# Transposing the layers' operands by DMA, token by token, instead of on TensorE

## The chip, the cores and the metric

The kernel runs on one core of a Trainium2 chip. The metric is device time in microseconds (us); lower is better. Three executions of the kernel before took 1181.19, 1182.12 and 1182.57 us, median 1182.12 us.

## The reference

Top-32 attention over 4 batches, 8 heads, 576 positions and 64 dimensions; its output, 2304 tokens by 512, passes through two layers with 2048 hidden columns each.

```python
scores = scale * np.matmul(q, k.transpose(0, 1, 3, 2))
kth = np.partition(scores, -top_k, axis=-1)[..., -top_k:-top_k + 1]
scores = np.where(scores >= kth, scores, -1000000000.0)
...
x = attention.transpose(0, 2, 1, 3).reshape(B * S, H * D)      # 2304 x 512
h = np.maximum(x @ moe_w_in, 0.0);  x = (h * h) @ moe_w_out    # first layer
h = x @ moe2_w_in                                             # second layer
out = (h * np.clip(h + 3.0, 0.0, 6.0) / 6.0) @ moe2_w_out
```

q, k and v are float32; the four weight matrices arrive as float64.

## The kernel before, in words

Every product keeps more than half precision: an operand is scaled by a power of two and split into two float16 parts, high and low, and a product is high*high + high*low + low*high, three matmuls for one (`PRODS`).

The 2304 tokens are cut into 20 blocks (four of 128 tokens and one tail of 64 in each batch), and these into 18 units of 128 tokens; two units consist of two tails each. Attention goes by tiles: 144 of them, eight for a block (one head each) or four for a tail (two heads each). A tile (`attend`) is scores on TensorE (line 769), their copy on ScalarE (775), seven VectorE passes for the 32 largest (783, 788, 791), a mask on GpSimd (808), the exponential on ScalarE (813), its two parts (819, 823, 824), a transposing DMA into wT (828), and 14 small matmuls with v (842).

When the tiles of a block are done, `x_operand` makes the first layer's input: ScalarE copies the block out of PSUM (912), four float32 transposes on TensorE turn it (921), ScalarE squares it (927), four matmuls with ones16 add the squares over the 512 columns, token by token (932), VectorE takes the largest (936) and a power of two from it (263 to 265), ScalarE scales (965) and rounds (968), GpSimd subtracts (971). That fills the tile hl of the unit: columns on partitions, tokens along the free axis.

A layer (`group`, m is 0 or 1) runs in four groups of four slices f of 128 hidden columns. For a slice, `up` makes 12 matmuls of 128x128 (1091): the hidden columns of 128 tokens. After the four slices follow the activation on ScalarE (and VectorE in the second layer), rounding (1113) and subtraction (1116) into ghl. Then `acc` multiplies by the second matrix, again slice by slice. In the second layer ghl is stationary and 512 columns of the weight move, three matmuls a slice (1134). In the first layer the weight is stationary, block by block, and the 128 tokens of ghl move: 12 matmuls a slice (1126), so that its result stands with columns on partitions, as the second layer's input must stand. `x2_operand` then squares it (1010), adds up (1016), scales (1028, 1029) and splits it (275, 279) straight from PSUM into hl, over the first input.

The order of the work is not that of the source. Every step is a task with an engine, an assumed cost, the tasks it needs, and the buffers that it takes and frees. `Plan.run` goes through them as through events in time; when an engine is free it takes, of the tasks that are ready and whose buffers are free, the one with the smallest key, `offset + slope * position` from the table `PRIO`. The engines run what comes out, each strictly in that order, and so does the queue of SyncE (SP), which issues all DMAs. A task of SP has latency 2.0 in the plan, the transposes into wT have `WLAT = 4.5`.

Of the kernel before, what the change touches and what calls it, by code (L numbers as in the profile page):

```python
# [134 lines left out]
def tile_topk_attention_moe_moe2(  # L135
# [36 lines left out]
    ones16 = const.tile([P, P], BF16, name="ones16")  # L172
    nc.gpsimd.memset(ones16, 1.0)
# [57 lines left out]
    pool("ghl", GBUFS, [P, 2, 512], F16)  # L231
    pool("m", 4, [P, TOPK], F32, st)
# [3 lines left out]
    for name, n in (("nb", NBUFS), ("kb", 2), ("ss", 6), ("sck", 1), ("scv", 1), ("scq", 2), ("qinv", 2), ("xy", 2), ("scx", 6),  # L236
                    ("px", 6), ("sc2", 4), ("p2", 2), ("r", 6), ("pm", 2), ("sm", 2), ("ca", 2), ("oc", 2)):
        scalar(name, n)
# [645 lines left out]
    def x_operand(i):  # L884
# [21 lines left out]
        def copy():  # L906
            box["x"] = x = take("x")
            a_ = T["av", i]
            for t in range(ntl):
                for hh in range(2 if tail else 1):  # L910
                    rows = slice(hh * TAIL, hh * TAIL + TAIL) if tail else slice(0, P)
                    nc.scalar.activation(x[0:n, 2 * t + hh if tail else t, :], a_[rows, t * D:(t + 1) * D], AF.Copy,  # L912
                                         scale=box["rv"][rows, t:t + 1])

        def flip():
            if o == 0:
                T["hl", u] = take("hl")
            box["pt"] = take("misc", "pt").rearrange("p (c n) -> p c n", c=KD)[:, :, 0:n]
            x = box["x"].rearrange("p h d -> p (h d)")
            for c in range(KD):  # L920
                nc.tensor.transpose(box["pt"][:, c, :], x[0:n, c * P:(c + 1) * P], ident[0:n, 0:n])

        def part(a):
            return T["hl", u][:, a, :, o:o + n]

        def square():
            nc.scalar.activation(part(1).bitcast(BF16), box["pt"], AF.Square)

        def total():
            box["pn"] = take("h", "pnx")[:, 0:n]  # L930
# [3 lines left out]
        def scale():  # L934
            y = take("xy")
            nc.vector.tensor_reduce(y, box["pn"], axis=AX.X, op=ALU.max)
            T["sx", i], T["px", i] = take("scx"), take("px")
            scale_pair(y, T["px", i], EXP_P, T["sx", i])
# [6 lines left out]
        t3 = task("ACT", 1.6, ("xcopy", first[i]), copy, deps=[t2, *avs], alloc=["x"])  # L945
        free("rv", t1, t3)
        free("av", avs[0], t3)
        t4 = task("PE", 0.44 if not tail else 0.3, ("xflip", first[i]), flip, deps=[t3, hl_task.get(u)],
                  alloc=["misc"] + (["hl"] if o == 0 else []))
        hl_task.setdefault(u, t4)  # L950
        free("x", t3, t4)
        t5 = task("ACT", act(4 * n), ("xsquare", first[i]), square, deps=[t4])
        t6 = task("PE", mm(KD, n), ("xtotal", first[i]), total, deps=[t5], alloc=["h"])
        t7 = task("DVE", 0.65, ("xscale", first[i]), scale, deps=[t6], alloc=["xy", "scx", "px"])
        free("h", t6, t7)
        free("xy", t7, t7)
        scale_task[i] = t7
        if (SX if i else SX0) == "d":
            l_, = split(4 * n, lambda: box["pt"], [lambda: part(0)], [lambda: part(1)], lambda: T["sx", i], "d",
                        (("xhigh", first[i]), ("xlow", first[i])), [t7])  # L960
            free("misc", t4, l_)
        else:
            def evac():
                box["y"] = take("f", "y").rearrange("p (c n) -> p c n", c=KD)[:, :, 0:n]
                nc.scalar.activation(box["y"], box["pt"], AF.Copy, scale=T["sx", i])

            def high():
                nc.scalar.activation(part(0), box["y"], AF.Copy)

            def low():  # L970
                nc.gpsimd.tensor_tensor(part(1), box["y"], part(0), op=ALU.subtract)

            t8 = task("ACT", act(4 * n) + 0.09, ("xevac", first[i]), evac, deps=[t7], alloc=["f"])
            free("misc", t4, t8)
            t9 = task("ACT", act(4 * n), ("xhigh", first[i]), high, deps=[t8])
            l_ = task("POOL", gps(4 * n), ("xlow", first[i]), low, deps=[t9])
            free("f", t8, l_)
        opd_task.setdefault((0, u), []).append(l_)

    def x2_operand(u):  # L980
# [19 lines left out]
        def bank(i):  # L1000
            w_ = P if n == P else 2 * P
            return acc_t.rearrange("p b n -> p (b n)")[:, 0:KD * w_].rearrange("p (c n) -> p c n", c=KD)[
                :, :, off[i]:off[i] + nof[i]]

        def part(i, a):
            return T["hl", u][:, a, :, off[i]:off[i] + nof[i]]

        def square(i):
            box["ss", i] = take("ss")
            nc.scalar.activation(part(i, 1).bitcast(BF16), bank(i), AF.Square, accum_out=box["ss", i],  # L1010
                                 **({"scale": T["px", i]} if several else {}))

        def total():
            box["pn"] = take("h", "pnx")[:, 0:1]
            for i in us:
                nc.tensor.matmul(box["pn"], ones32, box["ss", i], start=i == us[0], stop=i == us[-1])
# [15 lines left out]
        if several:  # L1032
# [3 lines left out]
            for i in us:  # L1036
                free("scx", scale_task[i], t1, *opd_task[0, u])
        sq = [task("ACT", act(4 * nof[i]), ("ysquare", pos[1, u, 0]), lambda i=i: square(i), deps=[t1, acc_task[0, u]], alloc=["ss"])
              for i in us]
        t3 = task("PE", 0.25, ("ytotal", pos[1, u, 0]), total, deps=sq, alloc=["h"])  # L1040
        for t_ in sq:
            free("ss", t_, t3)
# [3 lines left out]
        for i in us:  # L1046
            lows += split(4 * nof[i], lambda i=i: bank(i), [lambda i=i: part(i, 0)], [lambda i=i: part(i, 1)],
                          lambda i=i: T["px", i] if several else box["s"], "d", (("yhigh", pos[1, u, 0]), ("ylow", pos[1, u, 0])), [t4])
        opd_task[1, u] = lows
# [10 lines left out]
        for b_ in range(1 if n == P else 2):  # L1060
            free(f"acc{b_}", acc_task["first", 0, u], *lows)
# [10 lines left out]
    def group(m, u, g):  # L1072
# [45 lines left out]
        def acc(fi, chunks):  # L1118
            f = g * GF + fi
            gl = [box["g"][:, d, fi * n:(fi + 1) * n] for d in range(2)]  # L1120
            if m == 0:
                w_ = P if n == P else 2 * P
                flat_ = acc_t.rearrange("p b n -> p (b n)")
                for c in range(KD):
                    for a, d in PRODS:
                        nc.tensor.matmul(flat_[:, c * w_:c * w_ + n], wt[1][:, f, a, c * P:(c + 1) * P], gl[d],  # L1126
                                         start=(f, a, d) == (0, 0, 0) and c * w_ % 512 == 0,
                                         stop=f == KF - 1 and (a, d) == PRODS[-1], skip_group_check=True)
            else:
                for ch in chunks:  # L1130
                    rows = min(P, n - ch * P)
                    o_ = acc_t[0:rows, 1 if n == P else ch, :]
                    for a, d in PRODS:
                        nc.tensor.matmul(o_, gl[d][:, ch * P:ch * P + rows], wt[3][:, f, a, :],  # L1134
# [300 lines left out]
```

## Time and profile before

| | |
|---|---|
| median of three executions | 1182.12 us |
| the profiled execution | 1180.5 us, span 1178.7 us |
| PE (matmuls) | 1051.4 us busy, 89% |
| DVE | 988.8 us, 84% |
| ACT | 925.6 us, 79% |
| POOL | 835.3 us, 71% |
| mean granted TensorE clock | 0.979 |

The span runs from the first to the last instruction; the execution lasts 1.8 us longer. An engine's busy time is the time in which at least one of its instructions is shown; a matmul's length contains the way through the array, so the distance from one start to the next tells what it costs when they follow closely. The first 200 us, in which the weights are converted, and the last 80 us differ from what lies between.

### The profile page before, as it was taken

Reading aid. Unit: us, or ns where it says so; the run is one execution under the profiler, and the core shown is the slowest. Engines: PE = TensorE matmul, PEld = TensorE weight load, DVE = VectorE, ACT = ScalarE, POOL = GpSimd, SP = SyncE. Lnnn points to the kernel's source line nnn. Section 1 sums busy time; section 2 is a strip of 40 time slices with the busy share of each in tenths; the row PEclk is TensorE's granted clock in tenths of the full one; section 3 lists DMA queues with packets and bytes.
Section 4 is the critical chain, followed back from the end, with each engine's and each line's share of the span. In section 5 each row is a group of like instructions: output and inputs, shape, how many; then the busy total and the mean of one; then the engine's idle time right before and its main releaser. Section 6 shows DMA issues by size and latency. Waiting matters only on the chain.

```text
span 1178.7 us, 36919 instructions
## 1 busy us (share of the span) xinstructions
PE 1051.4 (89%) x14792; PEld 862.5 (73%) x14792; DVE 988.8 (84%) x2319; ACT 925.6 (79%) x1868; POOL 835.3 (71%) x1113
## 2 busy tenths in 40 slices
PE   2375688878999999999999999999989999999998
PEld 1232336776788788889787978888777978888885
DVE  4989899998995999999989999999978999998101
ACT  6589599899798878788888878888887787877432
POOL 5858868699775677777867787786766778777321
PEclk9997699988999999999999999999999999999999
DMA  9888754423554343445464443445463334333100
GB/s 235 234 249 244 225 156 119 104 48 65 90 97 102 79 75 55 75 74 98 78 118 84 71 74 56 72 62 92 86 110 55 66 65 80 62 60 61 12 11 19
DMA packets 276764, 112.50 MB, mean 95 GB/s; under 512 B 257520, under 2 KB 265712, under 8 KB 276592
## 3 DMA queue, kind: packets, MB, share of 16 engines
q1 hardware_dynamic: 276592, 110.14, 45.2%
q8 instruction: 116, 1.90, 0.7%
q14 instruction: 56, 0.46, 0.1%
HBM read 48.23 MB, written 4.72 MB: 45 GB/s over the span
## 4 chain that ended last, share of the span: by engine, by line
PE 53%; ACT 18%; DVE 9%; POOL 8%; issue 6%; DMA 5%; SPq 1%; ACTq 0%; DVEq 0%; POOLq 0%
PE hb L1091 21%; PE acc L1134 12%; PE acc L1126 11%; PE sp L769 4%; PE av L842 3%; POOL E L808 2%; ACT E L813 2%; DVE W L788 2%; ACT x L912 2%; POOL wc L823 2%; ACT S L775 2%; DVE m L791 1%; DVE cv L364 1%; DMA kT<-kn 1%; ACT w L541 1%
## 5 line engine op out<-in xcount | busy, mean ns | idle before, releaser
L1091 PE MATMUL hb<-hl,w 128*128 128x128 f16 x6912 | 456.2, 219 | 4.8 <-ACT stg L410 1.4
L1091 PEld LDWEIGHTS <-w 128*128 128x128 f16 x6912 | 411.4, 98 | 50.7 <-issue 6.4
L791 DVE MAX8 m<-W 128x8 f32<-128x576 f32 x432 | 326.0, 755 | 8.3
L1126 PE MATMUL acc<-ghl,w 128*128 128x128 f16 x3456 | 243.5, 221 | 5.3 <-ACT ghl L1113 2.6
L1134 PE MATMUL acc<-w,ghl 128*128 128x512 f16 x864 | 231.5, 379 | 11.7 <-DVE hl L279 7.5
L808 POOL TENSOR_TENSOR E<-S,E 128x576 f32<-128x576 f32 x144 | 204.3, 1419 | 48.5 <-ACT E L805 42.1
L1116 POOL TENSOR_TENSOR ghl<-r,ghl 128x512 f16<-128x512 f32 x144 | 169.4, 1177 | 93.5 <-ACT ghl L1113 85.3
L1126 PEld LDWEIGHTS <-w 128*128 128x128 f16 x3456 | 209.7, 99 | 17.6 <-issue 7.0
L788 DVE MATCH_REPLACE8 W<-m,W 128x576 f32<-128x576 f32 x288 | 213.8, 742 | 0.0
L823 POOL TENSOR_TENSOR wc<-E,wc 128x512 f16<-128x512 f32 x144 | 168.0, 1166 | 39.6 <-ACT wc L819 39.0
L775 ACT ACTIVATE S<-sp 128x576 f32<-128x576 f32 x144 | 93.5, 649 | 48.1 <-POOL E L808 40.0
L813 ACT ACTIVATE E<-E,scalars,scl 128x576 f32<-128x576 f32 x144 | 125.1, 869 | 4.4 <-POOL E L808 4.3
L805 ACT ACTIVATE E<-S,scalars 128x576 f32<-128x576 f32 x144 | 111.8, 776 | 19.0 <-DVE scalars L800 14.9
L783 DVE MAX8 m<-S 128x8 f32<-128x576 f32 x144 | 107.9, 750 | 18.9 <-ACT S L775 18.3
L769 PE MATMUL sp<-kT,qT 128*128 128x288 f16 (+1 forms) x640 | 100.1, 298 | 24.8 <-ACT S L775 20.0
L1134 PEld LDWEIGHTS <-ghl 128*128 128x128 f16 x864 | 74.9, 99 | 56.0 <-issue 16.0
L788 DVE MATCH_REPLACE8 W<-m,S 128x576 f32<-128x576 f32 x144 | 107.0, 743 | 0.0
L1106 DVE SCALAR_TENSOR_TENSOR r<-r,hb 128x512 f32<-128x512 f32 x72 | 49.0, 680 | 67.6 <-ACT r L1100 66.7
L1113 ACT ACTIVATE ghl<-r 128x512 f16<-128x512 f32 x144 | 90.5, 629 | 17.4 <-DVE r L1106 12.6
L819 ACT ACTIVATE wc<-E 128x576 f16<-128x576 f32 x144 | 98.5, 684 | 1.3
L795 POOL TENSOR_SCALAR scalars<-m,scl 128x1 f32<-128x1 f32 x144 | 38.5, 269 | 81.5 <-ACT E L813 32.2
L769 PEld LDWEIGHTS <-qT 128*128 128x128 f16 (+1 forms) x640 | 54.9, 103 | 51.8 <-issue 34.4
(130 smaller groups left out, 1493.5 us busy)
## 6 DMA issues: line engine op xcount, KB each, us to landing
w<-in_moe_w_in_dram SPq DMA_DIRECT2D x32, 512.0 KB, 4.9
w<-in_moe_w_out_dram SPq DMA_DIRECT2D x29, 512.0 KB, 4.4
out_dram<-o SPq DMA_DIRECT2D x16, 256.0 KB, 2.1
qf<-in_q_dram SPq DMA_DIRECT2D x31, 128.0 KB, 2.7
stg<-in_k_dram SPq DMA_DIRECT2D x12, 256.0 KB, 2.9
stg<-in_v_dram SPq DMA_DIRECT2D x12, 256.0 KB, 3.2
wT<-wc SPq DMA_TRANSPOSE x144, 3.2
stg<-in_moe_w_out_dram SPq DMA_DIRECT2D x6, 256.0 KB, 3.3
```

Source lines behind the costliest of these rows:

```text
L769: nc.tensor.matmul(dst, qT[:, 2 * ((2 * hp + hh) % 4) + a, 0:M], kflat[:, hh * SPAD + c * HALF:hh * SPAD + (c + 1) * HALF], start=a == 0, ...
L775: nc.scalar.activation(T["S", s].rearrange("p (c n) -> p c n", c=2), T["sp", s][:, :, 0:HALF], AF.Copy)
L788: nc.vector.match_replace(out=T["W", s], in_to_replace=m[:, 8 * c - 8:8 * c], in_values=T["S", s] if c == 1 else T["W", s], imm_value=-3.0e38)
L791: nc.vector.max(m[:, 4 * r:4 * r + 8], T["W", s])
L805: nc.scalar.activation(T["E", s], T["S", s], AF.Relu, bias=T["kb", s], scale=-FAR)
L808: nc.gpsimd.tensor_tensor(T["E", s], T["S", s], T["E", s], op=ALU.subtract)
L813: nc.scalar.activation(T["E", s], T["E", s], AF.Exp, bias=T["nb", s], scale=T["scl", ("q", i, half)][:, hp % 2:hp % 2 + 1], accum_out=T["s ...
L823: nc.gpsimd.tensor_tensor(wc[:, S + TAIL:], e[:, 0:S - TAIL], wc[:, 0:S - TAIL], op=ALU.subtract)
L1091: nc.tensor.matmul(box["h"][:, fi * n:(fi + 1) * n], wt[2 * m][:, kk * 4 + f // 4, a, f % 4 * P:(f % 4 + 1) * P], hl[:, c, kk, 0:n], start ...
L1116: nc.gpsimd.tensor_tensor(flat(box["g"][:, 1]), flat(box["r"]), flat(box["g"][:, 0]), op=ALU.subtract)
L1126: nc.tensor.matmul(flat_[:, c * w_:c * w_ + n], wt[1][:, f, a, c * P:(c + 1) * P], gl[d], start=(f, a, d) == (0, 0, 0) and c * w_ % 512 == ...
L1134: nc.tensor.matmul(o_, gl[d][:, ch * P:ch * P + rows], wt[3][:, f, a, :], start=f == 0 and (a, d) == (0, 0), stop=f == KF - 1 and (a, d) = ...
```

## The change

Both operands are now split while tokens lie on partitions, and turned afterwards by one transposing DMA for each (128 tokens x 2 parts x 512 columns, float16).

In `x_operand` the four TensorE transposes go. ScalarE squares the copied block in SBUF with a sum along each row (a reading of the accumulator more), one small float32 matmul with ones32 adds over the tokens (the sum of all squares takes the place of the largest), the VectorE reduction goes, the block is scaled in place, rounded, subtracted into the new buffer xh, and SP issues the transpose from xh into hl. In `acc` the first layer now does as the second: ghl stationary, 512 weight columns moving, three matmuls a slice. In `x2_operand` the split writes xh too, and a second transposing DMA fills hl. There is one buffer xh; of wT there are two instead of three. hl is taken at the copy and no longer at the transpose. The table PRIO has other numbers in every row, and so the order of all engines is another one; two of its rows are shown.

```diff
-    ones16 = const.tile([P, P], BF16, name="ones16")
-    nc.gpsimd.memset(ones16, 1.0)
...
+    pool("xh", XHBUFS, [P, 2, 512], F16)
...
+        def square():
+            box["xh"] = take("xh")
+            box["ss"] = take("ss")
+            nc.scalar.activation(box["xh"][0:n, 0].bitcast(BF16), rows(), AF.Square, accum_out=box["ss"][0:n])
+
+        def total():
+            box["pn"] = take("misc", "pnx")[:, 0:1]
+            nc.tensor.matmul(box["pn"], ones32[0:n, :], box["ss"][0:n], start=True, stop=True)
...
+        def scaled():
+            nc.scalar.activation(rows(), rows(), AF.Copy, scale=T["sx", i][0:n])
+
+        def high():
+            nc.scalar.activation(box["xh"][0:n, 0], rows(), AF.Copy)
+
+        def low():
+            nc.gpsimd.tensor_tensor(box["xh"][0:n, 1], rows(), box["xh"][0:n, 0], op=ALU.subtract)
+
         def flip():
-            if o == 0:
-                T["hl", u] = take("hl")
-            box["pt"] = take("misc", "pt").rearrange("p (c n) -> p c n", c=KD)[:, :, 0:n]
-            x = box["x"].rearrange("p h d -> p (h d)")
-            for c in range(KD):
-                nc.tensor.transpose(box["pt"][:, c, :], x[0:n, c * P:(c + 1) * P], ident[0:n, 0:n])
...
-            for c in range(KD):
-                nc.tensor.matmul(box["pn"], ones16, part(1).bitcast(BF16)[:, c, :], start=c == 0, stop=c == KD - 1)
...
+            nc.sync.dma_start_transpose(out=T["hl", u].rearrange("p a c n -> p (a c) n")[:, :, o:o + n],
+                                        in_=box["xh"][0:n].rearrange("p a n -> p (a n)"))
...
+        l_ = task("SP", 1.25, ("xflip", first[i]), flip, deps=[t10], lat=WLAT)
+        free("xh", t5, l_)
...
+        def flip():
+            nc.sync.dma_start_transpose(out=T["hl", u].rearrange("p a c n -> p (a c) n"),
+                                        in_=box["yh"].rearrange("p a n -> p (a n)"))
...
+            lows += split(DM, lambda r=rows(i): acc_t[r, 0, :], [lambda r=rows(i): box["yh"][r, 0]],
+                          [lambda r=rows(i): box["yh"][r, 1]], lambda i=i: (T["px", i] if several else box["s"])[rows(i)],
+                          "d", (("yhigh", pos[1, u, 0]), ("ylow", pos[1, u, 0])), [t4])
+        t6 = task("SP", 1.25, ("yflip", pos[1, u, 0]), flip, deps=lows, lat=WLAT)
...
-            if m == 0:
-                w_ = P if n == P else 2 * P
-                flat_ = acc_t.rearrange("p b n -> p (b n)")
-                for c in range(KD):
-                    for a, d in PRODS:
-                        nc.tensor.matmul(flat_[:, c * w_:c * w_ + n], wt[1][:, f, a, c * P:(c + 1) * P], gl[d],
...
+            o_ = acc_t[0:n, m, :]
+            for a, d in PRODS:
+                nc.tensor.matmul(o_, gl[d], wt[2 * m + 1][:, f, a, :], start=f == 0 and (a, d) == (0, 0),
+                                 stop=f == KF - 1 and (a, d) == PRODS[-1])
...
-WTB = 3
+WTB = 2
+XHBUFS = 1
...
-    "up0": (568.05, 3.995),
-    "up1": (500.02, 46.668),
...
+    "up0": (668.30, 0.933),
+    "up1": (894.69, 0.154),
```

ScalarE's queue at the last unit's first input, before: x is the copied block, pt the turned one, y the scaled one, hl the unit's operand; r and ghl belong to the layers.

```order
L1010 ACTIVATE hl,scalars<-acc 128x512
L1113 ACTIVATE ghl<-r 128x512
L912 ACTIVATE x<-av,rv 128x64 x8
L275 ACTIVATE hl<-acc,scalars 128x512
L1100 ACTIVATE r<-hb,bias_82,scalars 128x512
L927 ACTIVATE hl<-pt 128x512
L1113 ACTIVATE ghl<-r 128x512
L965 ACTIVATE y<-pt,scalars 128x512
L968 ACTIVATE hl<-y 128x512
```

The same place of the changed kernel (line 922 squares, 933 scales, 936 rounds; 996 is the square of the unit before, for its second layer):

```order
L913 ACTIVATE x<-av,rv 128x64 x8
L1105 ACTIVATE ghl<-r 128x512
L922 ACTIVATE xh,scalars<-x 128x512
L933 ACTIVATE x<-x,scalars 128x512
L936 ACTIVATE xh<-x 128x512
L1092 ACTIVATE r<-hb,bias_80,scalars 128x512
L1105 ACTIVATE ghl<-r 128x512
L996 ACTIVATE xh,scalars<-acc 128x512
```

The unit's first input now stands closed together, and the split of the unit before, which stood around it, comes behind it.

SP's queue at the end of the program, before: the transposes of the last tiles into wT, and the last stores.

```order
L730 DMA_TRANSPOSE qT<-kn 128x8x128
L828 DMA_TRANSPOSE wT<-wc 128x9x128 x7
L1214 DMA out_dram<-o 128x512
L828 DMA_TRANSPOSE wT<-wc 128x9x128 x5
L1214 DMA out_dram<-o 128x512 x3
```

And of the changed kernel (line 942 is the transpose of a first input, 1004 that of a second one):

```order
L1004 DMA_TRANSPOSE hl<-xh 128x8x128
L827 DMA_TRANSPOSE wT<-wc 128x9x128 x2
L942 DMA_TRANSPOSE hl<-xh 128x8x128
L827 DMA_TRANSPOSE wT<-wc 128x9x128 x2
L1195 DMA out_dram<-o 128x512
L827 DMA_TRANSPOSE wT<-wc 128x9x128 x3
L942 DMA_TRANSPOSE hl<-xh 128x8x128
L1004 DMA_TRANSPOSE hl<-xh 128x8x128
L1195 DMA out_dram<-o 128x512
L1004 DMA_TRANSPOSE hl<-xh 128x8x128
```

Two transposes for a unit stand among those of the tiles, on a queue that had none of them.

## Rows read from the trace of the kernel before

**Rows 1.** The page: busy time of the engines, and the chain's shares.
```profile
PE 1051.4 (89%) x14792; PEld 862.5 (73%) x14792; DVE 988.8 (84%) x2319; ACT 925.6 (79%) x1868; POOL 835.3 (71%) x1113
PE 53%; ACT 18%; DVE 9%; POOL 8%; issue 6%; DMA 5%; SPq 1%; ACTq 0%; DVEq 0%; POOLq 0%
```

**Rows 2.** Stretches: start:end, length, PE PEld DVE ACT POOL busy, clock, DMA, GB/s.
```profile
0.00:200.00 200.00, 114.86 (x746) 63.60 (x747) 170.34 (x378) 156.31 (x304) 149.21 (x177) 0.91 0.75 208
...
400.00:500.00 100.00, 98.96 (x1461) 83.14 (x1460) 94.48 (x221) 80.91 (x165) 73.78 (x102) 1.00 0.40 69
...
1000.00:1085.00 85.00, 84.71 (x1277) 72.13 (x1275) 81.04 (x179) 67.14 (x133) 62.39 (x79) 1.00 0.34 60
...
1100.50:1178.70 78.20, 72.63 (x940) 57.59 (x936) 9.87 (x25) 27.71 (x49) 17.87 (x17) 0.99 0.03 12
```

**Rows 3.** PE's waits from 200 us on: us in total, times, longest.
```profile
PE acc L1134 <- DVE hl L279: 7.5, 10, 0.9
PE sp L769 <- ACT S L775: 5.5, 4, 3.6
```

**Rows 4.** PE in order of time: start, length, instructions, count.
```profile
1118.29 0.83 PE L1126 MATMUL acc<-ghl,w 128*128 128x128 f16 x12
1118.96 0.83 PE L1091 MATMUL hb<-hl,w 128*128 128x128 f16 x12
...
1151.92 0.81 PE L1134 MATMUL acc<-w,ghl 128*128 128x512 f16 x3
1152.57 2.17 PE L1091 MATMUL hb<-hl,w 128*128 128x128 f16 x36
...
1168.42 6.64 PE L1134 MATMUL acc<-w,ghl 128*128 128x512 f16 x30
```

**Rows 5.** PE in order of time around transposes and sums.
```profile
1056.41 0.60 PE L921 MATMUL pt<-ident,x 128*128 128x128 f32 x4
1056.85 0.81 PE L1134 MATMUL acc<-w,ghl 128*128 128x512 f16 x3
1058.17 0.39 PE L932 MATMUL pnx<-hl,ones 128*128 128x128 bf16 x4
1058.39 0.57 PE L842 MATMUL av<-vv,wT 128*128 128x64 f16 x14
```

**Rows 6.** All engines in order of time: the last unit's sum of squares.
```profile
1141.98 0.60 ACT L1010 ACTIVATE hl<-acc 128x512 bf16<-128x512 f32 x1 [3.12 <-PE acc L1134]
1142.47 0.19 ACT L1010 ACTIVATION_READ_ACCUMULATOR hl<-acc 128x1 f32 x1
...
1142.72 0.38 PE L1016 MATMUL pnx<-scalars,ones 128*128 128x1 f32 x2
...
1142.96 1.46 PE L1134 MATMUL acc<-w,ghl 128*128 128x512 f16 x6
...
1145.18 0.75 DVE L279 SCALAR_TENSOR_TENSOR hl<-acc,scalars,hl 128x512 f16<-128x512 f32 x1 [0.54 <-ACT hl L275]
```

**Rows 7.** All engines: from the last tile to the last unit's first input.
```profile
1100.02 0.57 PE L842 MATMUL av<-vv,wT 128*128 128x64 f16 x14
1100.43 0.83 PE L1091 MATMUL hb<-hl,w 128*128 128x128 f16 x12
...
1101.01 1.73 ACT L912 ACTIVATE x<-av,rv 128x64 f32<-128x64 f32 x8
...
1102.63 0.60 PE L921 MATMUL pt<-ident,x 128*128 128x128 f32 x4
...
1108.08 1.16 POOL L971 TENSOR_TENSOR hl<-y,hl 128x512 f16<-128x512 f32 x1 [1.47 <-ACT hl L968]
```

**Rows 8.** Transposes into qT: SP's time in ns, least, median, most; landing in us.
```profile
L730 SPq DMA_TRANSPOSE qT<-kn x40: 1194/1232/2200, 7.7 to 1025.0; - x40
...
DMA to landing us min/median/max: 2.7/3.1/5.4
```

**Rows 9.** Who waited for a transpose into wT: us, times.
```profile
  PEld L842: 0.9, 2
```

More of the change, by code (lines that the diff above doesn't have):

```diff
@@ L907, in copy @@
             box["x"] = x = take("x")
+            if o == 0:
+                T["hl", u] = take("hl")
             a_ = T["av", i]
@@ L944, in x_operand @@
         avs = [av_tasks[i, t] for t in range(ntl)]
[L945 removed]
+        t3 = task("ACT", 1.6, ("xcopy", first[i]), copy, deps=[t2, *avs, hl_task.get(u)],
+                  alloc=["x"] + (["hl"] if o == 0 else []))
+        hl_task.setdefault(u, t3)
         free("rv", t1, t3)
         free("av", avs[0], t3)
[L948 to L949 removed]
@@ L950, in x_operand @@
[L950 to L956, printed above, removed]
-        scale_task[i] = t7
[L958 to L977, printed above, removed]
@@ new lines, in x_operand @@
+        t5 = task("ACT", act(H * D), ("xsquare", first[i]), square, deps=[t3], alloc=["xh", "ss"])
+        t6 = task("PE", 0.2, ("xtotal", first[i]), total, deps=[t5], alloc=["misc"])
+        free("ss", t5, t6)
+        t7 = task("DVE", 0.34, ("xscale", first[i]), scale, deps=[t6], alloc=["scx", "px"])
+        free("misc", t6, t7)
+        scale_task[i] = t7
+        t8 = task("ACT", act(H * D) + 0.09, ("xevac", first[i]), scaled, deps=[t7])
+        t9 = task("ACT", act(H * D), ("xhigh", first[i]), high, deps=[t8])
@@ L1059, in x2_operand @@
         free("p2", t4, t5)
-        for b_ in range(1 if n == P else 2):
-            free(f"acc{b_}", acc_task["first", 0, u], *lows)
+        free("acc0", acc_task["first", 0, u], *lows)
     PRODS = ((0, 0), (0, 1), (1, 0))
@@ new lines @@
+    "qflip": (-1853.07, 8.317),
+    "qk": (-107.90, 1.290),
+    "evac": (-234.65, 0.662),
+    "topk": (301.64, 0.948),
+    "bias": (-1723.17, 0.048),
+    "lowest": (299.95, 1.000),
+    "below": (164.49, 1.525),
+    "mask": (-161.55, 1.964),
+    "expo": (58.25, 1.189),
+    "whigh": (667.72, 2.141),
+    "wlow": (812.95, 0.224),
+    "wflip": (-102.44, 0.805),
+    "av": (609.90, 0.441),
+    "xinv": (-211.49, 3.990),
+    "xscales": (-221.33, 3.583),
+    "xcopy": (-212.46, 0.097),
+    "xflip": (335.99, 3.918),
@@ new lines @@
+    "xsquare": (23.27, 0.207),
+    "xtotal": (-357.75, 0.055),
+    "xscale": (184.03, 11.039),
+    "xevac": (-411.77, 1.057),
+    "xhigh": (-2455.71, 0.319),
+    "xlow": (355.78, 0.352),
+    "common": (420.79, 5.138),
+    "ysquare": (2109.22, 0.583),
+    "ytotal": (-237.40, 1.777),
+    "yflip": (-429.37, 0.932),
+    "yscale": (262.86, 0.157),
+    "yhigh": (-121.73, 0.079),
+    "ylow": (174.25, 0.109),
+    "whole": (-351.50, 4.507),
+    "up0": (668.30, 0.933),
+    "up1": (894.69, 0.154),
```

238 lines of the change are left out of this document (95 added, 143 removed).

## The prediction

> **What bounds the kernel now.** I read the profile's page first, then busy time by stretches, then what PE waited for, then single places in order of time. The page says that PE is busy 89% of the span, DVE 84%, and that PE holds 53% of the chain that ended last [rows 1]. By stretches there are three kernels in one. In the first 200 us PE is busy 114.86 us; the weights are being converted, and PE is not the limit. From 200 us to the last attention tile PE is nearly full: 98.96 of 100 us in one stretch, 84.71 of 85 in the last one, while DVE stands at 94.48 and at 81.04 of 85 [rows 2]. So PE binds there, with DVE a few per cent behind it. The last 78.2 us hold no attention: PE 72.63, DVE 9.87, ACT 27.71 [rows 2]. The clock is at its full 2.4 GHz in all of these but the first. PE's largest waits after 200 us are small, 7.5 and 5.5 us [rows 3]. Work taken from PE is therefore worth its time, if DVE can follow and if the new transfers do not make PE wait.
>
> **What PE loses.** Each slice of the first layer's second product was 12 matmuls of 128 columns; the next work starts 0.67 us later (1118.29 to 1118.96). A slice of three matmuls of 512 columns starts its successor after 0.65 us (1151.92 to 1152.57); more exactly, thirty such matmuls last 6.64 us, and since three of them last 0.81 where their successor starts after 0.65, some 0.16 of that is the last one's way through the array, so (6.64 - 0.16)/30 = 0.216 us each and 0.648 a slice [rows 4]. Columns are the same in number, 12 x 128 = 3 x 512, so this part brings only 0.022 us a slice: 18 units x 16 slices = 288, times 0.022, is 6.3 us. The weight loads fall to a quarter, but they lay beside the matmuls already, else 12 of them could not follow each other in 0.67 us; I give them nothing.
>
> Four transposes take PE 0.44 us (1056.41 to 1056.85) and the four matmuls of the sums 0.22 us (1058.17 to 1058.39) [rows 5]. For 20 blocks that is 8.8 and 4.4 us; the four tails are half as wide, which I neglect. In place of the sums comes one float32 matmul onto one column, shown as two, 0.24 us (1142.72 to 1142.96) [rows 6]: 20 x 0.24 = 4.8 us. PE's sum: 6.3 + 8.8 + 4.4 - 4.8 = 14.7 us less.
>
> **What the other engines gain or lose.** ACT reads an accumulator after each new square, 0.19 us [rows 6], times 20 is 3.8 us; its copies and roundings stay as many, with SBUF as the source in place of PSUM, and in the four tails they work on 64 rows of 512 instead of 128 of 256. ACT had 19 us free in 100 [rows 2], but attention's chain runs through it tile by tile. I charge 3 us of the end for that; the bounds are 0 (hidden) and 8 (all of it, and the tails' longer rows, at one square of 0.60 for each of four tails' steps). DVE loses a reduction for each block, nothing that decides.
>
> **The two transfers.** The nearest rows have the same shape, the transposes into qT: SP is held for 1.23 us (2.20 at most), and the data land 3.1 us later (2.7 to 5.4) [rows 8]. I add both, 4.3 us. 38 of them hold SP for 47 us of a span in which it mostly waits; behind a waiting one on that queue stand the transposes into wT and the loads of q. Whether PE sees the 4.3 us hangs on what stands between.
>
> First input: from the end of the last matmul with v (1100.43, when the next starts) to the end of the subtraction (1108.08 + 1.16 = 1109.24) it was 8.8 us [rows 7]. Without the transposes (0.60) and with the transfer it is 8.8 - 0.6 + 4.3 = 12.5 us. By the order of the changed kernel there stand on PE, between the last tile of the last unit and its first `up`, 7 slices of `up` and 12 of `acc`: 7 x 0.67 + 12 x 0.648 = 12.5 us. It just covers. Counted in the same way for the others, two units of the first 200 us have 8.3 and 9.8 us, eight have 12.5 to 15.7, seven more than 20. Before, the last unit had 8.1 us for 8.8. So I take no wait, and keep the case in which the chain is longer as a rival.
>
> Second input: from the square to the end of the split it was 1141.98 to 1145.93, 4.0 us [rows 6]; with the transfer 8.3 us. In the changed order at least 11 slices of `up` and 10 of `acc`, 13.9 us, or about as much stand between the last `acc` of a unit and its second layer (before, 4.4 us were the least). Hidden, with 5 us to spare.
>
> At this place the Trainium skill speaks against the change. "VectorE: DVE Perf Modes", section "Rules for kernel authors", says to transpose 128x128 on TensorE if the destination may be PSUM, and its section "The three transpose paths" gives 390 ns there against 1309 ns for the DMA. By it, the eight blocks of one such transfer would land after 10.5 us (an estimate from that page), and the first input's chain would be 20 us. The rows disagree with that for a whole transfer: eight blocks land in 3.1 us [rows 8], though four on PE cost only 0.44 us, so the rule's order holds and its distance doesn't.
>
> Two buffers for wT instead of three: PE's loads waited 0.9 us in all for a transpose into wT [rows 9]. A tile comes every 7 to 8 us in the mean (144 by 1100 us); a buffer is held from the start of its transpose until its matmuls are done, 4.3 us and PE's delay, and with two buffers that may be two tiles long. I take 0; the bounds are 0 and some 10 us, if as many tiles as now waited for the split (10 of [rows 3]) waited 1 us each.
>
> **The end.** In the changed order more is left for PE after the last tile: 55 slices of `up` and 66 of `acc` against 51 and 56, that is 79.6 against 70.5 us, where the 16 old `acc` slices count 0.67. The stretch after it was 78.2 us, so 7.7 more than its work; now it would be 87.3. To end 14.7 us earlier, attention has to finish 24 us earlier. PE's work before that point is less by as much. DVE must do its work in that shorter time: at 94.5% busy over 885 us it would come to 97% in 861. That is possible but narrow, and the reason why I don't expect more.
>
> **The sum.** 14.7 less on PE, 3 back for ACT: 12 us. On the profiled execution, 1180.5 - 12 = 1168.5 us (its span is 1178.7). The median of the runs shown is 1.6 us above it; 1182 - 12 = 1170 us.
>
> **Rivals.**
> - *More is saved.* With the longer covers the waits for the split and for the score copies, 7.5 and 5.5 us [rows 3], go too: 1170 - 13 = 1157 us. For it: in the new order the split's readers stand farther apart. Against: the first of these waits comes from PE's own buffer, which is the same.
> - *DVE takes over as the bound.* Attention's end moves by only half of the 24 us, because DVE is at 95% in the last stretch (81.04 of 85), and the 9 us more behind it eat the rest: -12 + 9 = -3, and with less, nothing: 1179 to 1184, 1182 us. For it: DVE's share; against it: DVE's stretches at 94% contain waits of its own for PE.
> - *The first input comes late.* Place: PE at a unit's first `up`, where all that follows on PE queues behind it, tiles' scores too, and through them DVE. The price is the lack of cover: with a chain of 14.3 us instead of 12.5 the lacks add up to 5.9 + 4.5 + 1.8 + 1.5 + 0.4 + 0.2 = 14 us over the 17 units, as much as PE saves; that is the point from which it decides. With landing at the 5.4 us and SP's 2.2 that the rows show as most [rows 8], 3.3 us more, the chain is near 16 and the lacks about 28 us: 1170 + 28 - 10 (the two in the first 200 us, where PE has room, count little) = 1188 us. For it: ACT and GpSimd run other work in between, as the 8.8 us contain; SP's queue is strict. Against: 3.1 is the median of 40.
> - *The transfers lie open*: wherever PE's work up to the need is itself held up by the unit's result, no cover counts, and each unit pays 3.7 us (4.3 - 0.6) for its first input and 4.3 for its second: 18 x 8.0 = 144, so 1170 + 144 = 1314 us. The rule of the Trainium skill's page "VectorE: DVE Perf Modes" points this way. Against it: strict order on PE, with 12.5 us or more of other work in between at nearly all units.
> - *The change does less than it says*, if 512 columns run no faster than four times 128: 6 us of the 14.7 are lost, 1176 us. The successors' distances in [rows 4] are read at four places only, so it stays within the forecast's own range.
>
> **How the numbers follow.** Forecast 1170 (own range 1160 to 1178) 0.48; more saved 0.14; DVE bound 0.18; first input late 0.18; transfers open 0.02. What a measurement can tell from no change is about 0.2%, 2.4 us: faster means below 1179.7, slower above 1184.5. Faster: 0.48 + 0.14 + 0.06 of the DVE case = 0.68. Same: 0.11 of the DVE case and 0.02 of the late input = 0.13. Slower: the rest, 0.19. Range 1155 to 1189: below it lies about 0.05, above it the open transfers and half of the late inputs, 0.1.
>
> **What would show it.** Right: PE's busy time near 1036 us; `acc` of the first layer at 0.65 us a slice; the last tile's matmuls near 1077 us and some 87 us behind them; no idle time of PE in front of `up` that a DMA into hl ends. Wrong: such idle time, eight times 2 us or more; or DVE busy over 97% from 1000 us on with the last tile after 1090 us; or PE's largest waits naming wT. A transfer into hl that lands later than 5 us in the median would make the forecast wrong by itself.

## The result and the profile after

The changed kernel takes 1166.8 us in the median of four executions (1166.5 to 1168.8); the kernel before took 1182.3 us beside it. The ratio is 0.9874, with a 95% interval of 0.9860 to 0.9887: 15.5 us less, where 12 were forecast. The profiled execution of the changed kernel was the slowest of its four (1168.8 us, span 1167.0 us, clock 0.98), so the two profiles, which are compared below, differ by 11.7 us of span and show a little less than the medians do.

The page, busy time and the chain's shares; they answer to [rows 1].

```profile
PE 1037.1 (89%) x12076; PEld 743.5 (64%) x12076; DVE 981.5 (84%) x2299; ACT 926.9 (79%) x1888; POOL 835.5 (72%) x1112
PE 37%; DVE 21%; ACT 17%; POOL 10%; issue 6%; DMA 6%; SPq 2%; POOLq 0%; ACTq 0%; DVEq 0%
```

PE has 14.3 us less to do (1051.4 before). The other engines' busy time hardly moved. The chain goes through DVE more often and through PE less, while PE's share of the span stayed at 89%.

The stretches of the changed kernel; columns as in [rows 2]. The last tile's matmuls start at 1081.1 us here, at 1100.0 before.

```profile
0.00:200.00 200.00, 118.70 (x870) 70.82 (x871) 171.68 (x380) 155.66 (x302) 153.88 (x181) 0.92 0.78 217
200.00:1081.50 881.50, 837.59 (x10345) 615.98 (x10344) 799.34 (x1895) 740.86 (x1533) 662.59 (x913) 0.99 0.48 87
1081.50:1167.00 85.50, 80.86 (x870) 56.71 (x866) 10.47 (x25) 30.34 (x54) 18.97 (x18) 1.00 0.08 20
...
400.00:500.00 100.00, 96.54 (x1203) 72.14 (x1201) 93.83 (x220) 81.73 (x162) 76.81 (x107) 1.00 0.45 76
981.00:1066.00 85.00, 83.40 (x1059) 62.76 (x1057) 80.01 (x181) 70.47 (x141) 63.71 (x81) 1.00 0.42 77
```

And of the kernel before, the stretch from 200 us to the last tile, as one row.

```profile
200.00:1100.50 900.50, 863.87 (x13116) 741.34 (x13114) 808.61 (x1917) 741.60 (x1517) 668.22 (x920) 0.99 0.43 78
```

With these, PE's idle time (length less busy) can be set against [rows 2], stretch by stretch: 85.1 us before and 81.3 after in the first 200 us; 900.5 - 863.9 = 36.6 and 881.5 - 837.6 = 43.9 up to the last tile; 78.2 - 72.6 = 5.6 and 85.5 - 80.9 = 4.6 behind it. In all 2.6 us more idle, and 14.3 less busy: 11.7. The last row of the first table is attention's last stretch here, as 1000 to 1085 us was before: both end 15 us before the last tile's matmuls. DVE is busy for 80.01 us of it, 81.04 before. Its share hardly moved, so whether it is the limit has to be tested by taking work from it, which is done below.

PE's largest waits from 200 us on (us, times, longest), then the wait of the small matmul that adds up the squares. They answer to [rows 3].

```profile
PE sp L768 <- ACT S L774: 7.6, 9, 2.2
PE acc L1115 <- POOL ghl L1108: 4.9, 3, 2.5
PE acc L1115 <- ACT o L1187: 4.0, 7, 1.6
...
PE pnx L926 <- ACT xh L922: 1.6, 4, 0.6
```

None of PE's waits names a transfer into hl or wT. Of the two waits that the longer covers might have removed, the one for the split fell from 7.5 us to 2.0 (line 278) and the one for the copies of the scores rose from 5.5 to 7.6; those for ghl and for the copy o of a result made up for the rest.

The last unit's first input, all engines in order of time (start, length, what; in brackets the idle time before it and what ended it). It answers to [rows 4 to 7].

```profile
1081.09 0.57 PE L841 MATMUL av<-vv,wT 128*128 128x64 f16 x14
1081.49 2.11 PE L1115 MATMUL acc<-w,ghl 128*128 128x512 f16 x9
1081.69 1.74 ACT L913 ACTIVATE x<-av,rv 128x64 f32<-128x64 f32 x8 [2.80 <-PE av L841]
...
1083.80 0.68 ACT L922 ACTIVATE xh<-x 128x512 bf16<-128x512 f32 x1
...
1084.11 0.81 PE L1115 MATMUL acc<-w,ghl 128*128 128x512 f16 x3
1084.32 0.25 ACT L922 ACTIVATION_READ_ACCUMULATOR xh<-x 128x1 f32 x1
1084.75 0.28 PE L926 MATMUL pnx<-scalars,ones 128*128 128x1 f32 x2
1084.89 0.83 PE L1083 MATMUL hb<-hl,w 128*128 128x128 f16 x12
...
1085.51 0.72 ACT L933 ACTIVATE x<-x,scalars 128x512 f32<-128x512 f32 x1 [0.95 <-DVE scalars L264]
...
1086.26 0.63 ACT L936 ACTIVATE xh<-x 128x512 f16<-128x512 f32 x1
...
1086.97 1.16 POOL L939 TENSOR_TENSOR xh<-x,xh 128x512 f16<-128x512 f32 x1 [1.72 <-ACT xh L936]
...
1088.15 1.24 SPq L942 DMA_TRANSPOSE hl<-xh  x1
...
1093.42 1.50 PE L1083 MATMUL hb<-hl,w 128*128 128x128 f16 x24
```

A slice of `acc` costs 0.64 us here (1084.11 to 1084.75) and the small matmul 0.14. The transpose is issued 6.5 us after the last tile's matmuls end. The operand is there 3.06 us after the issue began, at 1091.2; the unit's first `up` is the second half of the last row's 24 matmuls, and starts at 1094.1.

The transposes into hl: SP's time in ns (least, median, most) and landing, L942 for the first inputs and L1004 for the second ones. They answer to [rows 8].

```profile
L942 SPq DMA_TRANSPOSE hl<-xh x20: 1195/1233/1369, 131.4 to 1088.2; - x20
...
DMA to landing us min/median/max: 2.7/3.1/4.2
```

```profile
L1004 SPq DMA_TRANSPOSE hl<-xh x18: 1232/1236/2462, 210.2 to 1131.2; - x18
...
DMA to landing us min/median/max: 3.0/3.2/5.1
```

That is what the qT transposes showed. The landing counts from the start of the issue, so SP's 1.23 us lie within the 3.1 and are not to be added (the doubled transposes below show it again). All of PE's matmuls have records in this trace, so the n-th of line 1083 can be matched with the n-th of the changed program's order; that gives, unit by unit, how long before its first use each operand lies ready (its own landing in the trace, against the start of the unit's first `up`). First inputs: fifteen of 1.6 to 3.7 us, then 4.9, 8.3 and, for the first unit, 36.7. Second inputs: 2.4, 2.9, 3.5, 4.8, and fourteen of 5.2 or more. All are above zero, most of the first by little.

### The profile page after: what moved, and what is told of

Its sections match the earlier page's. It is cut to its first block, busy times and chain, and to the rows that moved or that the text cites. A ratio compares the mean times of both kernels' runs of the same rounds, so it can differ in the third digit from the quotient of the medians.

```text
span 1167.0 us, 31626 instructions
## 1 busy us (share of the span) xinstructions
PE 1037.1 (89%) x12076; PEld 743.5 (64%) x12076; DVE 981.5 (84%) x2299; ACT 926.9 (79%) x1888; POOL 835.5 (72%) x1112
## 4 chain that ended last, share of the span: by engine, by line
PE 37%; DVE 21%; ACT 17%; POOL 10%; issue 6%; DMA 6%; SPq 2%; POOLq 0%; ACTq 0%; DVEq 0%
PE acc L1115 16%; PE hb L1083 14%; DVE W L787 6%; DVE m L790 5%; POOL E L807 3%; PE sp L768 2%; ACT E L812 2%; DVE cv L363 2%; PE av L841 2%; DVE m L782 2%; ACT S L774 2%; DVE w L366 2%; DMA w<-in_moe_w_in_dram 1%; ACT x L913 1%; DMA kT<-kn 1%
## 5 line engine op out<-in xcount | busy, mean ns | idle before, releaser
L1115 PE MATMUL acc<-w,ghl 128*128 128x512 f16 x1728 | 451.8, 382 | 15.5 <-POOL ghl L1108 4.9
L1083 PEld LDWEIGHTS <-w 128*128 128x128 f16 x6912 | 415.8, 98 | 75.7 <-issue 6.1
L1115 PEld LDWEIGHTS <-ghl 128*128 128x128 f16 x1728 | 153.6, 99 | 130.4 <-issue 19.1
L804 ACT ACTIVATE E<-S,scalars 128x576 f32<-128x576 f32 x144 | 111.5, 774 | 12.3 <-DVE scalars L799 10.9
L841 PEld LDWEIGHTS <-wT 128*128 128x128 f16 (+1 forms) x2240 | 84.0, 102 | 21.7 <-issue 5.8
L841 PE MATMUL av<-vv,wT 128*128 128x64 f16 (+1 forms) x2240 | 90.9, 196 | 0.0
```

The costliest lines, as they stand in the source:

```text
L841: nc.tensor.matmul(out_[cols, t * D:(t + 1) * D], wT[0:kr, a, cols], vv[0:kr, vb, hh, c, :], start=n_ == 0, stop=n_ == len(prods) - 1)
L1083: nc.tensor.matmul(box["h"][:, fi * n:(fi + 1) * n], wt[2 * m][:, kk * 4 + f // 4, a, f % 4 * P:(f % 4 + 1) * P], hl[:, c, kk, 0:n], start ...
L1115: nc.tensor.matmul(o_, gl[d], wt[2 * m + 1][:, f, a, :], start=f == 0 and (a, d) == (0, 0), stop=f == KF - 1 and (a, d) == PRODS[-1])
```

## The experiments

Unless said otherwise, a kernel is the changed one in its own order with one edit; line numbers move by a few. Times are medians, and "us against the changed kernel" is a difference of medians; the intervals of the ratios are about 2 to 3 us wide to each side of such a difference. The letters of the theories are explained where the expectations first use them.

**PE's work put back, in two parts and together.** e1: the first layer's second product in 12 matmuls of 128 columns again.

```diff
+            if m == 0:
+                for c in range(KD):
+                    for a, d in PRODS:
+                        nc.tensor.matmul(o_[:, c * P:(c + 1) * P], gl[d], wt[1][:, f, a, c * P:(c + 1) * P], ...)
+                return
```

> The changed kernel with one thing undone: the first layer's second product again makes 12 matmuls a slice, each moving 128 columns (the stationary operand stays ghl), in the same order of all engines. Theory A (the gain is work taken from a PE that is full): 288 slices x 0.022 us = 6.3 us slower than the changed kernel, 1173 us. Theory B (the gain comes from the new order and from waits that it sheds, PE's work itself has room): 0 to 1.5 us slower, under 1168.5 us.

1175.7 us, ratio 0.9944 (0.9923 to 0.9964): 8.9 us more. A slice comes back to 0.67 us, PE is busy 7.6 us longer. The price of the forecast (6.3) lies within what the interval allows.

e2: four transposes and four sums a block, whose results nobody reads, ahead of the small matmul.

```diff
+            full = take("misc", "pnx")
+            for c in range(KD):
+                nc.tensor.transpose(full[:, c * P:c * P + n], rows()[:, c * P:(c + 1) * P], ident[0:n, 0:n])
+            sq_ = box["xh"][0:n, 0].bitcast(BF16)
+            for c in range(KD):
+                nc.tensor.matmul(full[:, 0:P], ones16[0:n, :], sq_[:, c * P:(c + 1) * P], start=c == 0, stop=c == KD - 1)
```

> The changed kernel, same order, with the four float32 transposes and the four matmuls of the squares put back on PE for each of the 20 blocks, as work whose result nobody reads. Theory A: 20 x (0.44 + 0.22) = 13.2 us less the four narrower tails, about 12.5 us slower than the changed kernel, 1179 us. Theory B: they hide in PE's idle time and in the longer covers, 0 to 3 us, under 1170 us.

1171.0 us, 0.9908 (0.9891 to 0.9925): 4.1 us more, not 12.5. And both together:

> Both of these at once: PE does all that it did before and the new small matmuls besides, in the new order. Theory A: 6.3 + 12.5 = 18.8 us slower than the changed kernel, 1186 us, and so 4 us slower than the kernel before, by the 20 small matmuls of 0.24 us. Theory B: at most 4 us slower than the changed kernel. If the sum comes out near 1182 us or below, the new order itself gave something.

1177.2 us, 0.9958 (0.9943 to 0.9972): 10.4 us more. The pages' busy rows of e2 and of both:

```profile
PE 1047.7 (90%) x12236; PEld 757.9 (65%) x12236; DVE 979.5 (84%) x2299; ACT 928.4 (79%) x1888; POOL 835.5 (71%) x1113
```

```profile
PE 1051.7 (90%) x14828; PEld 866.9 (74%) x14828; DVE 979.6 (83%) x2299; ACT 929.1 (79%) x1888; POOL 835.5 (71%) x1113
```

With both, PE is as busy as before the change (1051.4), and the kernel is still 5 us faster than before. So some 10 of the 15.5 us come by PE's work; the other 5 don't. In e2 only a part of 10.6 us more on PE reached the end. From the copy of the second block on, behind which 19 of the 20 blocks are turned, PE is busy 6.8 us longer than in the changed kernel (915.9 against 909.1), and idle 3.3 us less. The small matmul shows how work put back can fill a wait: PE's 1.6 us of waiting for the square went to 0.4. The clock helped too: between 200 and 300 us 0.95 was granted in e2's profile and 0.91 in the changed kernel's. Whether the work put back keeps it up isn't shown.

**The order's table alone.** The kernel before with the changed kernel's PRIO, nothing else.

> The kernel before, unchanged in its operations, with the changed kernel's table PRIO (so in another order than either). With all of PE's old work put back the changed kernel was still some 5 us faster than the kernel before. Theory E (that rest is the order, which starts the first unit's first layer earlier, when PE is not the limit): 1176 to 1179 us, and PE busy over 118 us in the first 200 us, as in the changed kernel. Theory F (the table only fits the operations that it came with; the rest comes from the new operand chains): 1182 us or slower.

1203.6 us, 1.0177 (1.0163 to 1.0191): 21.6 us slower than before. The first blocks are copied as early as in the changed kernel (120 and 211 us, before 175 and 219), but that is lost later; PE's wait for the copy of the scores grew threefold against [rows 3]:

```profile
PE sp L769 <- ACT S L775: 15.9, 11, 3.6
```

The table is no gain by itself. PE's busy time grew too, from 1051.4 to 1064.3 us, at a mean clock of 0.974 against 0.979. With the old table's numbers `Plan.run` stops on the changed kernel before all tasks have run, so the old order with the new operands is not measured. The 5 us therefore belong to the order and the operands' new path together.

**The transfers.** First both transposes into hl were issued twice, the second waiting for the first to land.

```diff
-            nc.sync.dma_start_transpose(out=T["hl", u]..., in_=box["yh"]...)
+            for _ in range(2):
+                nc.sync.dma_start_transpose(out=T["hl", u]..., in_=box["yh"]...)
```

> The changed kernel, same order, with each of the 38 new transposes into hl made twice; the second waits for the first to land, so an operand comes about 4.3 us later and SP is held some 4 us longer. Theory A (transfers covered, second inputs by 5 us, first inputs just so): second inputs cost nothing; first inputs lack 1.1 to 4.3 us at the eight units with short covers, together about 20 us: 1180 to 1190 us. Theory C (covers are longer than I counted, nothing is near its limit): 1167 to 1170 us. Theory D (the transfers already cost their time at every handover): 38 x 4.3 = 160 us slower.

1207.1 us, 1.0204 (1.0184 to 1.0224): 40 us more, far above what I had expected. Then each alone, the first input's and the second's:

> The changed kernel, same order, with only the 20 transposes of first inputs made twice (the second waits for the first to land). Both kinds doubled cost 40 us. Theory A (lack of cover at the first inputs): nearly all of it, 25 to 40 us, 1192 to 1207 us, with PE waiting in front of the first layer's `up` for a DMA into hl. Theory G (SP is held, and what stands behind it on its queue comes late): about half, 20 us, with PE and ACT waiting for wT, kT and q instead.

1189.7 us, 1.0066 (1.0053 to 1.0078): 22.9 us more.

> The changed kernel, same order, with only the 18 transposes of second inputs made twice. Theory A (5 us to spare): 0 to 4 us, 1167 to 1171 us. Theory G (SP held 18 times for some 4 us): about 18 to 20 us, 1185 us, without PE waiting for a DMA into hl.

1185.8 us, 1.0025 (1.0011 to 1.0039): 19 us more. The sum is that of both. Two waits with the first input's issued twice: PE's for the operand, and SP's own for the landing of the first of the two.

```profile
PE hb L1084 <- DMA hl<-xh: 8.1, 8, 2.2
```

```profile
SPq L943 <- DMA hl<-xh: 36.1, 20, 3.0
```

The second row tells when a transpose lands: SP issues the first of the two for 1.23 us and then waits 36.1/20 = 1.8 us for it, 3.0 us from start to landing. By their landings the operands come 3.4 us later in the mean, not the 4.3 that the expectation named. Of the 17 times to spare (without the first unit's) twelve are shorter than that, by 10 us in all. PE's wait for hl, 8.1 us in 8 places, fits; it is not the whole of 22.9. Two other things make up the rest. What stands behind the held SP comes late: PE's waits for kT, for the squares of k and v, and for wT are 16.1 us here and 5.9 in the changed kernel. And from the second block's copy on PE is busy 4.8 us longer with the same work, and less clock was granted (0.97 between 300 and 400 us, 0.98 between 800 and 900, where the changed kernel has 1.00).

For the second input the operand's own lateness is worth next to nothing (2.4 and 2.9 us to spare against 3.4), and PE waits 0.7 us for hl; but 19 us were measured. Most of them, 17, appear in steps of 2.6, 6.7, 4.8 and 3.0 us before the copies of four blocks out of twenty. The largest step, PE, ACT, and the clock in the stretch behind the wait (columns as in [rows 2]):

```profile
312.92 1.47 PE L1116 MATMUL acc<-w,ghl 128*128 128x512 f16 x6
318.06 0.58 PE L600 MATMUL pnq<-scalars,ones 64*128 64x1 f32 x2 [3.67 <-ACT kn L596]
318.57 1.46 PE L1116 MATMUL acc<-w,ghl 128*128 128x512 f16 x3
```

```profile
317.50 0.42 ACT L596 ACTIVATE kn<-qf 64x256 bf16<-64x256 f32 x1 [4.04 <-DMA kT<-kn]
```

```profile
317.80:324.50 6.70, 6.44 (x38) 3.95 (x39) 5.65 (x14) 5.26 (x12) 4.24 (x7) 0.50 0.20 45
```

ACT waits with the square of a new q, since the buffer kn is not yet free: the transpose out of it stands on SP's queue behind a doubled one, begins at 311.9 us (307.6 in the changed kernel) and lands 5.6 us later (3.4 there). PE sits idle for 3.7 us for this square, which is theory G. Then it works at half its clock, 1.2 GHz, until 324.5 us: three matmuls of 512 columns take 1.26 us to the start of the next work (318.57 to 319.83), not 0.65. So the wait is paid nearly twice. The steps of 4.8 and 3.0 us look alike: idle times of 2.9 and 3.0 us on PE, for a wT and a kT, and a fall to half the clock right behind. A third way leads through the one buffer xh. Held longer by a second input, it makes ACT wait with the square of a first one:

```profile
ACT xh L922 <- DMA hl<-xh: 4.6, 7, 1.4
```

The changed kernel has no such wait, and PE's at the small matmul is 4.7 us here instead of 1.6. From the second block's copy on, PE's idle time grew by 10.9 us and its busy time by 8.8. Each way is read from this trace; none was tested alone.

Doubling is more than there is. To see what the transfers cost as they are, both were made plain copies of the same bytes, unturned.

```diff
-            nc.sync.dma_start_transpose(out=T["hl", u].rearrange("p a c n -> p (a c) n"),
-                                        in_=box["yh"].rearrange("p a n -> p (a n)"))
+            nc.sync.dma_start(T["hl", u].rearrange("p a c n -> p (a c n)"), box["yh"].rearrange("p a n -> p (a n)"))
```

> The changed kernel in its own order, but both transfers into hl are plain copies of the same 256 KB instead of transposes, so that the operands stand unturned (this changes what is computed; the time shows what the turning costs). SP should be held for some 0.1 us instead of 1.23 us, 38 times, and the data should land about 1 us earlier. Theory A (the transfers as they are lie under other work on PE, only longer ones show): 1164 to 1168 us against 1167 of the changed kernel. Theory G (SP's queue already pays for each of them, as it did for the doubled ones, about half of the 1.1 us each that doubling cost): 38 x 0.55 = 21 us less, 1142 to 1156 us.

1167.0 us, 0.9877 (0.9860 to 0.9893): the same as the changed kernel, 0.2 us apart. The first inputs' copies:

```profile
L942 SPq DMA_DIRECT2D hl<-xh x20: 465/519/632, 129.6 to 1086.3; - x20
...
DMA to landing us min/median/max: 2.2/2.4/3.7
```

SP is held 0.52 us instead of 1.23 (I had expected 0.1), and the data land 2.4 us after the issue began instead of 3.1: each operand is ready 0.7 us earlier, and SP has 27 us less to do in all. Nothing comes of it. G is refuted for the transfers as they are, and the forecast's zero is shown within the 2 us or so that the runs can tell apart. Together with the doubled ones it shows a threshold, not a price per microsecond.

Third, the first inputs' transposes from ScalarE's queue.

```diff
-            nc.sync.dma_start_transpose(out=T["hl", u]...[:, :, o:o + n], in_=box["xh"][0:n]...)
+            nc.scalar.dma_start_transpose(out=T["hl", u]...[:, :, o:o + n], in_=box["xh"][0:n]...)
```

> The changed kernel, but the 20 transposes of the first inputs are issued by ScalarE's queue instead of SP's; the second inputs' stay on SP. SP has 20 x 1.23 = 25 us less to issue and none of the waits for GpSimd's subtraction in front of its other transposes (75 us of waits in the trace); ScalarE gets both, at 79% busy. Theory A (cover holds, SP's queue has room): no gain, and ScalarE's 25 us come through to PE at a fifth to a half: 1172 to 1182 us. Theory G (what stands behind a waiting transpose on SP's queue is late and costs): 1152 to 1164 us.

1196.5 us, 1.0125 (1.0109 to 1.0140): 30 us more, worse than either theory had. The relief for SP turned into a new wait, and PE's wait for ScalarE's copies of the scores doubled from 7.6 us:

```profile
SPq L827 <- DMA hl<-xh: 77.1, 13, 10.7
```

```profile
PE sp L768 <- ACT S L774: 15.6, 16, 3.5
```

Line 827 moves wc into wT and shares no tile with hl; yet SP waited there for ScalarE's transpose to land, 13 times. The Trainium skill, "DMA: Bandwidth & Descriptors", section "Silent corruption: two transposing streams in flight at once", says that the first transpose of a later stream must wait until the earlier stream has completed; the waits in the trace are of this kind. The run therefore doesn't tell what a freer SP alone is worth.

**DVE.** The third replacing pass on 512 of 576 columns, in the changed kernel and in the one before.

```diff
+                w_ = S if c < 3 else 512
-                nc.vector.match_replace(out=T["W", s], in_to_replace=m[:, 8 * c - 8:8 * c], ...)
+                nc.vector.match_replace(out=T["W", s][:, 0:w_], in_to_replace=m[:, 8 * c - 8:8 * c], ...)
```

> The changed kernel, same order, with the third replacement pass of each tile on VectorE running over 512 of 576 columns (so the last 8 of the 32 maxima may be taken from a slightly different set): 144 x 0.74 x 64/576 = 11.9 us less for DVE, nothing else. Theory A as I forecast it (PE binds, DVE a few per cent behind): 0 to 2 us faster, 1165 to 1167 us. Theory H (after the change DVE binds as much as PE, which is why PE work put back cost so little): 4 to 8 us faster, 1159 to 1163 us.

1166.2 us, 0.9865 (0.9851 to 0.9878): 0.6 us less.

> The kernel before in its own order, but the third of the three replacing passes of a tile works on 512 of 576 columns (the last 64 columns are left as they were, which changes what is computed): DVE does some 12 us less. Theory A (PE binds before the change, too): 1179 to 1184 us against 1182. Theory H (DVE held attention's end before the change, and taking work from PE paid only by the order): 1170 to 1176 us.

1180.2 us, 0.9984 (0.9975 to 0.9994): 1.3 us less than the kernel before. The shorter pass takes 676 ns instead of 743, 9.6 us in all and not the 12 of the expectations; DVE is busy 7.9 us less in the changed kernel and 9.0 in the one before. That is worth about one microsecond in either. H is refuted.

**ScalarE's share.** The first input's square twice.

```diff
+            for _ in range(2):
                 nc.scalar.activation(box["xh"][0:n, 0].bitcast(BF16), rows(), AF.Square, accum_out=box["ss"][0:n])
```

> The changed kernel with the square of every first input done twice (the second writes the same values again): ScalarE does 20 x (0.64 + 0.22) = 17 us more, and every first input's chain is 0.86 us longer, where the trace of the changed kernel leaves it 0.3 to 7.9 us before PE needs it (0.3, 0.8 and fifteen of 1.1 or more). Theory A (the forecast's price: four fifths of what ScalarE gets more comes through to the end): 1176 to 1182 us against 1167. Theory I (ScalarE's extra work lies in its own idle time, and the chain's slack takes the 0.86 us): 1166 to 1169 us.

1178.0 us, 0.9973 (0.9960 to 0.9985): 11 us more, as A's price had it, but not for A's reason:

```profile
PE pnx L927 <- ACT xh L923: 10.8, 16, 1.3
```

This wait was 1.6 us in the changed kernel; it grew by 9.2 us, and the two profiles lie 11.0 us apart. It is most of the loss. From the second block's copy on PE is also busy 3.7 us longer, with a fall of the clock (0.98 between 300 and 400 us) that the changed kernel doesn't have. The small matmul that adds up the squares stands in PE's strict order so close behind the tile that it starts as the square's sum is read. A look at the unit with the least to spare, in the changed kernel, shows both places where PE meets this chain:

```profile
985.13 1.46 PE L1115 MATMUL acc<-w,ghl 128*128 128x512 f16 x6
...
988.61 0.25 ACT L922 ACTIVATION_READ_ACCUMULATOR xh<-x 128x1 f32 x1
988.91 0.30 PEld L926 LDWEIGHTS pnx<-scalars,ones 128*128 128x128 f32 x2 [0.39 <-ACT xh L922]
988.91 0.38 PE L926 MATMUL pnx<-scalars,ones 128*128 128x1 f32 x2
...
993.82 1.35 SPq L942 DMA_TRANSPOSE hl<-xh  x1
...
998.59 1.62 PE L1083 MATMUL hb<-hl,w 128*128 128x128 f16 x26
```

The matmul starts 0.05 us behind the reading of the sum, and it starts within 0.07 us of it at 11 of the 20 blocks (from the starts and ends in the trace): there any delay of the square shows. The operand lands 3.2 us after its issue began, at 997.0, and is used at 998.6, so 0.86 us more leave it in time. (The expectation's 0.3 to 7.9 us count SP's time twice; they are 1.6 to 8.3.)

## Why the prediction was right, step by step

The sign and the mechanism were right, and so was the size of the whole: 1170 forecast, 1166.8 measured. Not all of its terms were, and that the whole came so close is in part luck: a term too large for the transposes and sums, and some 5 us of gain that were in no term, about cancel.

- *PE binds, and PE's work is the gain.* Right. PE's busy time fell by 14.3 us where the sum had 14.7 (1036 was named, 1037.1 measured), and 8 to 9 us off DVE bring one.
- *512 columns, 6.3 us.* Right: 8.9 when undone, with an interval that holds 6.3.
- *Transposes and sums, 8.8 + 4.4 us.* The step that failed in size. As busy time they are 10.6; put back, they cost 4.1. I had taken each microsecond of PE at its full price, and hadn't seen that work at this place fills a wait, nor that the clock differs between runs. How the 4.1 splits between the two is open.
- *The small matmul, 4.8 us.* From its start to PE's next 0.24 us in the median, 20 times, as forecast; at the last unit, where PE didn't wait, it is 0.14 (1084.75 to 1084.89).
- *ScalarE, 3 us.* Charged for a wrong reason. What costs is not its load but PE's wait for the square at the small matmul, 1.6 us of PE's waits now and 10.8 with a longer square. The prediction followed the chain to the first `up` and passed over the first place where PE needs something of it.
- *Transfers, 0.* Right, and no gain when they are 0.7 us shorter. The size of a transfer was wrong: "I add both, 4.3 us" counts SP's 1.23 us twice, since the rows' 3.1 us begin with the issue. A transfer takes 3.1 us; the first input's chain is 11.3 us, not 12.5, against a cover of 12.5, and the second's 7.1. So the zero didn't hang by as little as it said. At the last unit, for which it was reckoned, it came to 9.6 us from tile to landing against 12.4 to first use; over the units the medians are 14.1 and 17.1. The rival of the late first input lies 2 to 4 us away at most units: 3.4 us more for each cost 23 us, of which PE's wait for hl is 8.1, against 28 less 10 that the prediction had for 3.3 us. That these totals are near each other is chance.
- *Second input, 5 us to spare.* Too high for four of the units: 2.4, 2.9, 3.5 and 4.8 us, though the chain was reckoned 1.2 us too long.
- *Two buffers for wT, 0.* Right for PE, which never waited for one. The third buffer's loss appears on SP. Its wait for the matmuls that free a wT, before and after (us, times, longest):

```profile
SPq L828 <- PE av L842: 1.9, 1, 1.9
```

```profile
SPq L827 <- PE av L841: 35.2, 23, 4.4
```

- *The end.* The last tile came 19 us earlier, not 24, with 85.5 us behind it against 87.3 forecast. (With the 16 old `acc` slices at 0.67 the 70.5 us of that reckoning are 70.8.)
- *Left out.* Some 5 us of the gain remain with PE's work put back. In that kernel PE idles 1174.5 - 1051.7 = 122.8 us, before 127.3. This belongs to the order with the new path, and the runs don't separate the two.

Of the rivals, DVE as the bound fell by the last tile at 1081.1 us (its sign was one after 1090) and by the 0.6 us that 8 us less for DVE brought; the open transfers fell by the plain copies. "More is saved" named two waits of which only one shrank.

No run with the whole computation is faster than the changed kernel. The runs point at one: the small matmul one slice of PE's work later, which could return up to the 1.6 us of waits. It was not tried.

## What to carry to other kernels

When PE's stream is strict, follow a moved chain to every place where PE needs something of it, the small ones first: a matmul of 0.14 us set the price here, and a transfer of 3.1 us was free. A cover that just holds gives zero for the cost as it is and says nothing of a longer one, so test such a zero from both sides, by shortening and by lengthening; and then read from the trace what the longer one cost, since a held queue, a shared buffer and a fallen clock come with it. Check from where a view counts a time before adding another to it. And price work put on or taken from an engine by whether it stands where the engine waits.

## What was not expected of the hardware

- A plain copy of 256 KB within SBUF held SP 0.52 us and landed 2.4 us after its issue began; the transpose of the same bytes took 1.23 and 3.1. The Trainium skill, "Advanced Engine Details and Errata", section "X-Bar Transpose (TRN2)", has transposes as fast as regular DMAs; by these rows it is 0.7 us in 3.1 slower, and here it made no difference to the end.
- Transposes of two queues did not overlap: with 20 on ScalarE's queue no two were in flight together, and SP waited 77.1 us for those of ScalarE.
- PE idle for 2.9 to 3.7 us at a time in attention lost clock as well: in the run with the second inputs doubled, three such waits were each followed by a stretch at 1.2 GHz.
